# Low part of a fifth weight block by TensorE, with a new order table, in an attention and gated-projection kernel

## The chip, the cores and the metric

The kernel runs on one core of one Trainium2 chip. The metric is device time in microseconds (us) of one execution. The engines are named as the profile names them: PE is TensorE's matmul row, PEld its weight load, DVE is VectorE, ACT is ScalarE, POOL is GpSimd, SP is SyncE, which issues the DMAs.

## The reference

Four batches, eight heads of width 64, 768 positions. Each query sees the first 8 positions and the 96 up to itself, with a linear bias by distance. The heads' outputs are put side by side (512 wide), and a gated block follows:

```python
scores = scale * np.matmul(q, k.transpose(0, 1, 3, 2)) + bias
a = softmax(np.where(keep, scores, -1e9)) 
x = np.matmul(a, v)                                  # (4, 768, 512) after the transpose
gate = 1.0 / (1.0 + np.exp(-causal_conv(x, conv_w))) # 5 taps, per channel
out = (gate * (x @ w_val)) @ w_out                   # both weights 512 x 512
```

The two weights come as 64-bit floats. The kernel splits each into a high part and a low part of 32-bit type and makes three matmuls for each product (high by high, high by low, low by high).

## The kernel before

**Work and stages.** The 768 positions of a batch are cut into two phases of three blocks of 128, so there are eight phases (0 to 7). In each phase four groups (one pair of heads each) go through the attention; two groups make a pair, q = 0 to 15. Every piece of work is an operation with a key, added to a plan in `attention_moe`. The keys that this text uses:

- `Lrk`, `Lrq`, `LV`, `WL`: DMA loads of keys, queries, values and a weight block (line 582), issued by SP.
- `S u`: scores of three steps on PE (line 685). `AM s,j`: bias added and the row minimum taken, on DVE (line 693). `EX s,j`: exponential, on ACT (line 704).
- `RG q,k`: a small number added to four row sums (line 711, POOL or DVE). `RC q,k`: their reciprocal, DVE (line 714). `NM s,j`: the product with it, POOL or DVE (line 720).
- `PT q,k`: transposes on PE, as 12 small ones (line 737), or as 6 whole ones (line 734) where the unit before it on PE uses the whole array. `EV q,k,i`: their copy out of PSUM (line 326, ACT or DVE).
- `PV q,k`: product with the values, PE (line 765). `HI g` prepares the PSUM bank of group g for it (line 328 or 863); `HO g` saves four columns.
- `XH g`, `XL g`: high and low part of x (lines 326 and 872). `CV g,k`: tap k of the convolution (line 881, the first one often on ACT, line 883). `SG ph`: the gate's tanh, ACT.
- `VM ph,m,c`: three matmuls of x with block c of the first weight, PE (line 935). `GM ph,m`: gate times value, DVE (line 944). `GH`, `GL`: its high and low part. `OM ph,k,h,c`: three matmuls with block c of the output weight, PE (line 963). `OE`, `ST`: copy out and store.

**The weight blocks.** There are eight blocks of 128 rows, i = 0 to 3 of the first weight and 4 to 7 of the output weight. A block goes through `WA` (ACT, line 552), `W1`, `W2`, `W3` (DVE, lines 557, 562, 565), `W4` (line 571, POOL or DVE), and `WH`, the cast to the high part (`w_high`, line 591). Then the low part is made in one of two ways. For i < `PE_W` (line 618) it is `WS`, a sum in PSUM by TensorE (`w_sum`, lines 604 to 611), and `WP`, its copy out on ACT (`w_out`, line 326):

```python
nc.tensor.matmul(ps, ident, T["wh", i][:, :DM].bitcast(F32), start=True, stop=False)   # 609
nc.tensor.matmul(ps, units[:, 1], h[:, c], start=False, stop=False)                    # 610
nc.tensor.matmul(ps, units[:, 0], T["wr", i][:, :DM], start=False, stop=True)          # 611
```

For the others `WS` is a subtraction (`w_rest`, line 598) and `WP` an addition (`w_low`, line 602), both on POOL in this kernel. The buffers of the blocks are rings of two, so `W2` of block i waits for `WP` of block i-2. The first `OM` of phase 0 waits for `WP` 4 to 7 (line 1043).

**What sets the order.** `ORDER` lists every operation by the number in which it was added to the plan, with a letter where one of several engines was chosen (a ACT, v DVE, g POOL). The operations of one engine are issued in the order in which they stand there, and an engine takes them strictly in that order. `Plan.order` also works out where the plan expects PE to wait in the first 95 us and puts up to 12 filler matmuls there (lines 450, 458, 464). PSUM banks are rings too: `S u` needs the banks of `S u-1` back from its `AM`s, and `WS`, `VM` and `OM` share a ring of two ("moe").

Of the kernel before, what the change touches and what calls it, by code (L numbers as in the profile page):

```python
# [28 lines left out]
LAG, PV_SPLIT, U_VK, PE_W = 1, 1, 0.0, 4  # L29
WS_POS = (4, 4, 4, 4)  # L30
# [27 lines left out]
    396g 166a 417 418 395g 174 185 419 427 397g 428 420 398g 437 402a 438 421g 22 429 178 422 401a 179 233 426g 430
    11 180 175a 21 425g 311 431v 453 416 423g 432 454 262 404a 433g 457 403a 458 436g 187 439 435g 263 461 12 440
    462 182g 188 24 455 434g 234 1129a 23 189 424g 1135a 194 441v 1138a 1130 183g 177 312 1139 1127a 465 1140 186  # L60
    181g 13 1131 447a 29 448a 466 456 475 190g 313 1128 1136a 476 459 1398 442 485 467 443g 486 203 450a 1141 445g
    235 468 446g 1132 477 18 469g 1142 444g 449a 28 460 184g 1133 314 31 463 1126v 1137 478 470 1143 487 1152 479v
# [1286 lines left out]
```

## Time and profile before

| what | value |
|---|---|
| median of 3 runs | 251.1 us (250.1 to 251.37) |
| the profiled execution, whole time | 249.76 us |
| its span | 248.0 us |
| busy in the span: PE, DVE, ACT, POOL | 238.8, 213.4, 179.6, 130.4 us |
| filler and warm-up matmuls | 13 + 2 of line 450, and 15 more of lines 458 and 464 |

The span is what the profile sees; 1.76 us lie around it. All times in rows count from the span's start. PE is busy 96% of the span, but the first fifth of the span differs from the rest, so the page's shares are read by stretch.

### The profile page before, as it was taken

To read this page: it belongs to the slowest core of one execution; us is meant where nothing else is said; L and a number is where in the kernel's file an instruction comes from. 1 tells how busy PE (TensorE), PEld (TensorE's weight loads), DVE (VectorE), ACT (ScalarE), POOL (GpSimd) and SP (SyncE) were. 2 spreads that over 40 slices of the span, in tenths; PEclk is the share of its full clock that TensorE was granted. 3 is DMA by queue.
4 is the path that set the end of the run, shared out by engine and by line. 5 is a ranking of instruction groups with operands and counts; after the bars stand their busy time and mean duration, and the time that the engine had idled before them with its cause. 6 is when DMAs were issued, how large, how long until landed. Compare 5 with 4: busy or idle time off the path is not lost.

```text
span 248.0 us, 10366 instructions
## 1 busy us (share of the span) xinstructions
PE 238.8 (96%) x4037; PEld 204.7 (83%) x4041; DVE 213.4 (86%) x822; ACT 179.6 (72%) x600; POOL 130.4 (53%) x264
## 2 busy tenths in 40 slices
PE   8998788999999999999999999999999999999993
PEld 3556577888899888988899788898899889988993
DVE  3997999998979989898989989898979979989620
ACT  3999899998998488877967589886678388422202
POOL 6989999999317530364064533455419741810220
PEclk9999999999999999999999999999999999999999
DMA  5999598161298054529558289791079507200303
GB/s 181 401 397 386 200 336 284 36 187 52 61 306 306 3 186 186 167 100 272 187 172 256 84 272 345 221 312 48 7 261 402 200 25 227 73 4 0 127 8 134
DMA packets 23095, 45.94 MB, mean 185 GB/s; under 512 B 2688, under 2 KB 13696, under 8 KB 23040
## 3 DMA queue, kind: packets, MB, share of 16 engines
q1 hardware_dynamic: 23040, 45.21, 53.4%
q8 instruction: 34, 0.56, 0.9%
q14 instruction: 21, 0.17, 0.2%
HBM read 38.91 MB, written 6.29 MB: 182 GB/s over the span
## 4 chain that ended last, share of the span: by engine, by line
PE 80%; DVE 12%; POOL 4%; DMA 1%; issue 1%; ACT 0%; SPq 0%; DVEq 0%; POOLq 0%
PE o L963 26%; PE val L935 25%; PE x L765 11%; PE s L685 9%; PE pt L734 5%; PE pt L737 4%; DVE gate L881 3%; DVE t L693 3%; POOL p L720 3%; DVE wh L562 2%; DMA counts_i<-in_counts 1%; DVE xl L872 1%; DVE wy L557 1%; POOL wvh L328 1%; DVE wy L565 1%
## 5 line engine op out<-in xcount | busy, mean ns | idle before, releaser
L720 POOL TENSOR_SCALAR p<-p,rs 128x168 f32<-128x168 f32 (+1 forms) x152 | 66.3, 450 | 55.1 <-DVE rs L714 36.4
L704 ACT ACTIVATE p<-t,mins 128x168 f32<-128x168 f32 (+1 forms) x192 | 81.5, 430 | 13.8 <-DVE mins L693 12.2
L881 DVE SCALAR_TENSOR_TENSOR gate<-x,cwt,gate 128x384 f32<-128x384 f32 x128 | 76.2, 614 | 1.1
L693 DVE CUSTOM_DVE_ANT_0 t<-s,bias 128x168 f32<-128x168 f32 (+1 forms) x192 | 54.1, 318 | 7.6 <-PE s L685 7.5
L935 PE MATMUL val<-xh,wvh 128*128 128x384 f32 x128 | 44.4, 347 | 0.2 <-DVE gate L944 0.2
L326 ACT COPY a<-pt 128x384 f32<-128x384 f32 (+2 forms) x79 | 35.3, 473 | 11.7 <-PE pt L734 7.6
L935 PE MATMUL val<-xl,wvh 128*128 128x384 f32 x128 | 41.8, 327 | 0.0
L935 PE MATMUL val<-xh,wvl 128*128 128x384 f32 x128 | 41.7, 326 | 0.0
L963 PE MATMUL o<-woh,gh 128*128 128x512 f32 (+1 forms) x100 | 39.1, 391 | 0.0
L704 ACT ACTIVATION_READ_ACCUMULATOR p<-t,mins 128x1 f32 x192 | 37.6, 196 | 0.0
L963 PE MATMUL o<-woh,gl 128*128 128x512 f32 (+1 forms) x100 | 37.2, 372 | 0.0
L963 PE MATMUL o<-wol,gh 128*128 128x512 f32 (+1 forms) x100 | 37.1, 371 | 0.0
L765 PEld LDWEIGHTS x<-a,v 56*64 56x64 f32 (+1 forms) x2112 | 33.7, 135 | 4.0 <-issue 1.1
L685 PE MATMUL s<-rk,rq 64*64 64x168 f32 (+1 forms) x768 | 35.8, 304 | 1.1 <-issue 0.9
L765 PE MATMUL x<-a,v 56*64 56x64 f32 (+1 forms) x2112 | 35.8, 219 | 0.8 <-DVE x L863 0.7
L685 PEld LDWEIGHTS s<-rk,rq 64*64 64x64 f32 x768 | 25.8, 132 | 8.9 <-issue 6.0
L952 POOL TENSOR_TENSOR gl<-gate,gh 128x384 fp32r<-128x384 f32 x24 | 24.1, 1008 | 11.8 <-ACT gh L326 5.0
L935 PEld LDWEIGHTS val<-xh,wvh 128*128 128x128 f32 x128 | 24.2, 189 | 1.8 <-DVE gate L944 0.5
L935 PEld LDWEIGHTS val<-xl,wvh 128*128 128x128 f32 x128 | 24.2, 189 | 0.5 <-DVE xl L872 0.2
L935 PEld LDWEIGHTS val<-xh,wvl 128*128 128x128 f32 x128 | 24.2, 189 | 0.0
L944 DVE SCALAR_TENSOR_TENSOR gate<-gate,val 128x384 f32<-128x384 f32 x32 | 17.4, 549 | 4.7 <-PE val L935 4.5
L963 PEld LDWEIGHTS o<-wol,gh 128*128 128x128 f32 x100 | 18.9, 189 | 2.4
(101 smaller groups left out, 351.0 us busy)
## 6 DMA issues: line engine op xcount, KB each, us to landing
v<-in_vw SPq DMA_DIRECT2D x40, 384.0 KB, 5.6
rq<-in_qT SPq DMA_DIRECT2D x32, 192.0 KB, 5.3
rk<-in_kT SPq DMA_DIRECT2D x16, 252.0 KB, 4.8
out<-ob SPq DMA_DIRECT2D x15, 256.0 KB, 4.8
w<-in_wb SPq DMA_DIRECT2D x7, 512.0 KB, 5.8
again<-in_wb SPq DMA_DIRECT2D x7, 512.0 KB, 5.9
rk<-in_kT SPq DMA_DIRECT2D x16, 200.0 KB, 4.9
out<-ob SPq DMA_DIRECT2D x12, 128.0 KB, 1.8
```

Source lines behind the costliest of these rows:

```text
L326: nc.scalar.copy(dst, src)
L685: nc.tensor.matmul(T["s", step[g, k], j][half], T["rq", g][r, k * P + i * HQ : k * P + (i + 1) * HQ], T["rk", g][r, c0 : c0 + n], start=Tr ...
L693: nc.vector.tensor_tensor_reduce(out=t[:, :n], in0=T["s", s, j], in1=bias[:, h, :P] if n == P else bias[:, h, P:], op0=ALU.add, op1=ALU.mi ...
L704: nc.scalar.activation(p_of(s, j), T["t", s, j][:, :n].rearrange("p (c w) -> p c w", c=pieces(s)[0]), AF.Exp, bias=mins[:, s, j : j + 1], ...
L720: engine(e).tensor_scalar(out=pr, in0=pr, scalar1=rs, scalar2=1.0, op0=ALU.mult, op1=ALU.mult)
L734: nc.tensor.transpose(pt[n // 4][:, n % 4 * P : n % 4 * P + P], src, ident)
L765: nc.tensor.matmul(T["x", 2 * q + r][j * D : (j + 1) * D, c0 : c0 + HQ], v[rows, slot], a[rows, i, n * j + c], start=c == 0, stop=c == use ...
L881: nc.vector.scalar_tensor_tensor(out=gt, in0=src, scalar=w, in1=gt, op0=ALU.mult, op1=ALU.add)
L935: nc.tensor.matmul(T["val", ph, m], (wvh, wvh, wvl)[r][:, c, m * P : (m + 1) * P], woven((T["xh", g], T["xl", g], T["xh", g])[r][:, : size ...
L944: nc.vector.scalar_tensor_tensor(out=t, in0=t, scalar=1.0, in1=T["val", ph, m].rearrange("p (b a) -> p a b", a=2), op0=ALU.add, op1=ALU.mult)
L952: engine(e).tensor_sub(tile_of(("gl", ph, m), [P, HT], F32R, "gl", G_B)[:, :n], T["g", ph, m], T["gh", ph, m][:, :n])
L963: nc.tensor.matmul(T["o", ph, k, h], (T["gh", ph, c], T["gl", ph, c], T["gh", ph, c])[r][:, cols], woven((woh, woh, wol)[r][:, c])[:, h * ...
```

## The change

Two constants and the whole order table change:

```diff
-LAG, PV_SPLIT, U_VK, PE_W = 1, 1, 0.0, 4
-WS_POS = (4, 4, 4, 4)
+LAG, PV_SPLIT, U_VK, PE_W = 1, 1, 0.0, 5
+WS_POS = (0, 4, 4, 4)
 ORDER = """
-    114 0 118 1125 1134 140 2 3 120 1g 122 123 138a 130g 119 128g 149 141 124g 142 133g 131a 143 126a 8 229 125g
+    114 0 118 1124 140 3 2 120 122 123 136a 126g 134a 124g 132a 149 119 1g 142 8 125a 130g 127a 143 135g 7 228 131a
...
```

With `PE_W` 5, block 4 takes the first way: `WS 4` becomes three matmul forms on PE, `WP 4` a copy on ACT, `wr` of the block is written in the rounded 32-bit type. `WS_POS[0]` of 0 takes its PSUM bank from the ring ahead of `VM 0,0`, and the operation is added later, so all numbers between the two places fall by one. Decoded with that, the first part of the two tables reads as follows on each engine (loads of SP left out; blanks between key and numbers left out).

```
before, PE:   ... S4 PT0,2 PV0,1 PV0,2 S5 PT1,0 PT1,1 VM0,0,0 S6 PT1,2 PV1,0 PV1,1 PV1,2 PT2,0 VM0,1,0 VM0,0,1 VM0,1,1
              S7 PT2,1 VM0,0,2 VM0,1,2 VM0,1,3 PT2,2 VM0,0,3 PV2,0 PV2,1 S8 VM0,2,0 VM0,2,1 ... OM0,0,0,0 ...
after,  PE:   ... S4 PT0,2 PV0,1 PV0,2 PT1,0 S5 WS4 PT1,1 VM0,0,0 S6 PT1,2 PV1,0 PV1,1 PV1,2 PT2,0 VM0,0,1 VM0,1,0 VM0,1,1
              VM0,0,2 S7 PT2,1 VM0,0,3 VM0,1,2 VM0,1,3 PT2,2 PV2,0 PV2,1 S8 VM0,2,0 VM0,3,0 ... OM0,0,0,0 ...
before, DVE:  ... AM11,1 W14 RC1,0 W24 W34 RG1,1 AM12,0 RC1,1 AM12,1 AM13,0 AM13,1 W15 AM14,0 AM14,1 W25 W35 RG1,2 CV0,1 CV1,1
              AM15,0 CV1,2 CV0,2 AM15,1 AM16,0 XL0 AM16,1 RC1,2 AM17,0 AM17,1 CV1,3 CV0,3 CV1,4 CV0,4 HO0 XL1 RC2,0 HI2 HI3 RG2,1
              ... W26 W17 ... CV2,4 CV3,4 HI4 AM21,1 HI5 AM22,0 AM22,1 AM23,0 AM23,1 W27 GM0,0 GM0,1 RC3,0 ... W47 GL0,0 ... XL4 AM29,1
after,  DVE:  ... W12 RG0,1 ... W14 AM11,1 W24 RG1,0 RC1,0 W34 RG1,1 AM12,0 RC1,1 AM12,1 W15 AM13,0 AM13,1 RG1,2 AM14,0 AM14,1
              W25 W35 CV0,1 RC1,2 CV0,2 CV1,1 CV1,2 CV0,3 AM15,0 XL0 AM15,1 AM16,0 CV0,4 AM16,1 RG2,0 AM17,0 HI2 RC2,0 AM17,1 CV1,3
              XL1 CV1,4 HI3 ... W26 W17 ... CV2,4 CV3,4 AM21,0 HI4 HI5 AM21,1 AM22,0 AM22,1 AM23,0 AM23,1 GM0,0 GM0,1 RC3,0 W27
              AM24,0 AM24,1 GL0,0 ... W47 ... AM29,0 CV5,1 AM29,1 CV4,3 CV5,2 XL4
before, POOL: ... RG1,0 NM9,1 NM9,0 NM6,0 NM7,0 NM10,1 NM10,0 WH4 NM7,1 NM6,1 WS4 W44 W45 NM8,0 NM11,0 NM11,1 RG2,0 NM8,1 WP4
              ... WS5 ... WP5 WS6 W46 RG3,0 WP6 NM21,1 NM18,0 NM21,0 NM22,1 GH0,0 ... WS7 WP7 ...
after,  POOL: ... WH4 NM9,0 NM6,0 NM9,1 NM7,0 NM6,1 NM10,0 NM10,1 W44 NM11,0 NM8,1 W45 NM7,1 WH5 NM11,1 NM8,0
              ... WS5 ... WH6 ... WS6 NM17,0 W46 WP6 WP5 RG3,0 GH0,0 ... WH7 ... WS7 WP7 ...
before, ACT:  ... EX6,1 WP2 EX9,0 EX9,1 EV0,1,1 EX10,0 ...
after,  ACT:  ... WP2 EX6,1 EX9,0 EV0,1,1 EX10,0 EX9,1 ... EX13,1 EX16,0 WP4 EV1,1,0 ...
```

Over the whole table these move between engines: `WH` 1, 5, 6, 7 from ACT to POOL; `BIAS` (six of sixteen from POOL to ACT, three back); `RG 0,1`, `RG 1,0` and `RG 2,0` from POOL to DVE in this stretch, `RG 2,1` from DVE to POOL; `HO 0` from DVE to ACT. Later in the table eight more `EV` and the three `OE` of DVE go to ACT. On PE, `PT 1,1` now follows a unit of the whole array (`WS 4`), and further on two `PT`s leave the whole form and two others take it, so 22 `PT`s take the whole form where 21 did. On SP some loads of the head change places, and none is added: the two operations of block 4 issue no DMA.

## Rows read from the trace of the kernel before

**Rows 1.** Busy time by stretch; columns PE, PEld, DVE, ACT, POOL, clock, DMA share, GB/s.
```profile
0.00:46.50 46.50, 41.26 (x716) 27.71 (x720) 40.76 (x173) 40.76 (x141) 41.99 (x85) 1.00 0.80 292
46.50:243.70 197.20, 197.17 (x3320) 176.84 (x3321) 172.60 (x650) 138.14 (x458) 88.36 (x180) 1.00 0.49 161
```

**Rows 2.** Chain of waits that ended last, head alone: start, us, what.
```profile
22.32 0.20 POOL sm L711
22.55 0.18 DVE rs L714
...
43.52 0.07 DVE x L328
...
43.83 0.08 DVE x L328
...
44.90 1.10 DVE wh L562
```

**Rows 3.** Timeline of PE, 25 to 47 us: start, us, instruction, [idle before and its releaser].
```profile
25.75 1.32 PE L685 MATMUL s<-rk,rq 64*64 64x168 f32 x23
27.97 0.35 PE L685 MATMUL s<-rk,rq 64*64 64x168 f32 x1 [0.89 <-issue]
28.57 0.47 PE L737 MATMUL pt<-ident,p 64*128 64x64 f32 x8 [0.25 <-issue]
29.50 0.86 PE L737 MATMUL pt<-ident,p 64*128 64x64 f32 x12 [0.46 <-ACT a L326]
...
34.43 2.00 PE L765 MATMUL x<-a,v 64*64 64x64 f32 x120 [0.73 <-DVE x L863]
...
40.26 0.59 PE L737 MATMUL pt<-ident,p 64*128 64x64 f32 x12 [0.64 <-POOL p L720]
...
46.53 0.43 PE L935 MATMUL val<-xh,wvh 128*128 128x384 f32 x1 [0.16 <-DVE gate L944]
```

**Rows 4.** Timeline of PE: four fillers; the first matmuls of two weight blocks' sums.
```profile
7.65 1.05 PE L464 MATMUL ptf<-const-bfloat16-1.0 128*128 128x512 bf16 x4
...
10.49 1.12 PE L609 MATMUL wsum<-wh,ident 128*128 128x512 f32 x2
...
11.92 1.02 PE L609 MATMUL wsum<-wh,ident 128*128 128x512 f32 x2
```

**Rows 5.** Chain that ended last: one unit of small and one of whole transposes.
```profile
50.53 0.52 PE pt L737 x12
...
53.20 0.66 PE pt L734 x6
```

**Rows 6.** Groups of instructions of POOL, 0 to 60 us: busy us, mean ns, idle.
```profile
L720 POOL TENSOR_SCALAR p<-p,rs 128x168 f32<-128x168 f32 x38 | 17.9, 486 | 0.5 <-DVE rs L714 0.2
L598 POOL TENSOR_TENSOR wh<-wh,woh 128x512 f32<-128x512 f32 x4 | 5.1, 1282 | 0.0
...
L328 POOL CAST wvh<-wh 128x512 fp32r<-128x512 f32 x3 | 2.9, 961 | 0.0
...
L534 POOL TENSOR_SCALAR bias<-dist 128x168 f32<-128x168 f32 x4 | 2.1, 536 | 0.2
...
L328 POOL CAST woh<-wh 128x512 fp32r<-128x512 f32 x1 | 0.6, 605 | 0.0
```

**Rows 7.** Timeline of DVE around its one wait after the start.
```profile
20.76 0.44 DVE L557 TENSOR_SCALAR wy<-w 128x512 int32<-128x512 int32 x1
...
23.75 0.15 DVE L711 TENSOR_SCALAR sm<-sm 128x4 f32<-128x4 f32 x1
```

**Rows 8.** Line 562 (`W2`): duration ns shortest/median/longest, first and last start us.
```profile
L562 DVE SCALAR_TENSOR_TENSOR wh<-w,wy x8: 660/702/1194, 6.7 to 44.8; 128x512 int32<-128x512 int32 x7, 128x532 int32<-128x532 int32 x1
```

**Rows 9.** Timeline of POOL: `W4` of blocks 4 and 5 together.
```profile
28.80 2.51 POOL L571 TENSOR_TENSOR wr<-wls,wy 128x512 f32<-128x512 f32 x2
```

**Rows 10.** ACT: the end of `EX 9,1` on the timeline, and the group of `WP` 0 to 3.
```profile
20.34 0.19 ACT L704 ACTIVATION_READ_ACCUMULATOR p<-t,mins 128x1 f32 x1
...
L326 ACT CAST wvl<-wsum 128x512 fp32r<-128x512 f32 x4 | 2.3, 577 | 0.0
```

More of the change, by code (lines that the diff above doesn't have):

```diff
@@ L58 @@
[L58 to L62, printed above, removed]
@@ L128 @@
-    1766 1776 1771 1777 1772 1778
+    114 0 118 1124 140 3 2 120 122 123 136a 126g 134a 124g 132a 149 119 1g 142 8 125a 130g 127a 143 135g 7 228 131a
+    141 4 144 128g 138a 356 145g 129a 357 358 360 115 139a 361 362 364 146g 116 365 158 150 151 117 366 152 9 363
+    229 153 10 359 155g 227 367 147 368 154g 369 370 378 379 371 388 380 372v 137g 167 389 156 373 381 1133 376v 14
+    377g 148a 160 374g 15 382v 133a 161 375g 159 5 230 162 390 164g 383 163v 391 308 387g 157a 404 405 165 392g 406
@@ new lines @@
+    731g 1513 764 772 756g 1509 1504g 1229a 77 747 1514 1505g 1478 1510 774 1515 1234 55 1511a 1520 1484 1235 736a
+    1512g 1237a 1516 773 751 1230 1521 775 1517 246 1241 1518v 331 80 788 1519g 1238 790 1522 1490 1244v 757 765
+    1242 60 761g 1526 1243 1523 760v 1252v 776v 766v 1527 767 1524a 777 789 792 778g 281 738a 793 780g 739a 61 796
+    791 758g 282 797 759g 794 768g 247 779g 771g 283 800 770g 769v 332 801 781g 1247v 1528 782a 62 1248 802 1532
+    1249 798 783a 1529 1250 799 810 1533 1530a 811 820 1245a 1534 1255v 795 1251 333 67 822 821 812 1535 1253v 785a
@@ new lines @@
+    1559g 861 1564 337 1271a 1268 884 1568 834a 885 211 1278 1565a 1276 1573 1537 871 1566g 1277 1569 75 886 1272
+    1574 856g 888 862v 1287 872g 1570 835v 889 288 863 1571a 873 892 865g 875v 887 287 864g 893 289 212 876g 877v
+    251 1288a 866g 1282a 867v 76 874g 890 338 86 896 1291a 897 1575 213 891 906 1283 879a 1579 898 1280v 878a 1576
+    1292 908 907 1580 899 1293 81 1577a 339 1281 91 909 1294 1578 1581 880a 916 881a 1586 917 894 1295 1582 900v
+    1289a 901 1284 252 1583a 904g 1285 903g 895 340 93 918 1286 82 1593 1290 883a 932 1594 933 934 936 1587 882a
@@ new lines @@
+    905v 1595 937 1585 940 1588 98 902v 941 94 1596 214 919 1589 1279a 253 920g 1296a 910g 1304a 935 911 914v 341
+    915g 938 944 913g 945 292 946 954 99 955 947 912v 215 290 926a 964 948g 927a 1572 965 291 939 921 83 949 1590
+    924g 942 254 925g 1299v 1591g 1597 342 1307a 923g 1297a 1600 922g 1308 929a 950g 1309 966 1601 1592g 956 1607
+    1298 957 980 1602 1310 943 1608 958g 88 981 1598g 928a 959 1603 1300 1305a 100 962g 1609 982 1599v 951g 967 343
+    1604 984 1610 1605g 985 986 952v 1614 89 1606g 1611 101 988 1615 1612a 1301 105 983 1620 1306 1613g 217 987 989
@@ new lines @@
+    223 1017 1631 1034 298 1637 108 1022a 1644 296 1638g 1018v 257 1329a 1011g 1031 1639v 1332a 1008v 1647 1040
+    1341a 1041 1648 1330a 1050 1042 1654 1051 1060 1043 1649 1333 113 1645a 1655 1044g 1334 1023a 96 1650 1646g
+    1338a 1335 1052 1656 1053 1651 348 1019g 1045 1061 1020g 1652a 1331 1657 1021g 1024a 1661 1046g 1035 1658 1025a
+    258 1336 1054g 1339a 1653g 97 1659a 1340 225 349 1038 1342 1660g 1625 1062 1662 1346 1343 1039 1047g 1026a 1667
+    1344 1027a 1076 1663 1063 1077 1078 1080 1668 1064g 1055 1079 1065 1345 1059g 1664 1058g 1056v 1057g 1669 1355
@@ new lines @@
+    1695 1115g 1368 1373a 1104g 1701 1118a 1369 1106g 1696 1119a 1107g 1114v 1702 1116g 1370 111 1697 1117g 1672
+    1374 1693g 354 1678 1698 1703 1376 1121a 1699g 1708 1120a 1377 1700g 1371 355 1378 1709 1123a 1379 1122a 1704
+    1380a 1710 1388a 1705 307 1706a 1707v 305 306 1714 1383a 1391a 1384 1711 1392 1715 1712a 1393 1381a 1716 1394
+    1720 1385 1389a 1717 1382 1390 1721 1718a 1386 1722 1395 1723 1387 1727 1724a 1780 1728 1726 1734 1729 1735 1730
+    1736 1731 1737 1732v 1741 1738 1742 1733v 1739g 1748 1781 1743 1749 1744 1740v 1782 1750 1745 1713 1767 1751
@@ L129 @@
+    1725 1755 1719 1752 1773 1746v 1756 1753v 1747v 1761 1754v 1768 1762 1757 1783 1763 1758 1769 1759 1764 1760
+    1770 1765 1774 1771 1775 1766 1776 1772 1777 1778
 """.split()
```

114 lines of the change are left out of this document (45 added, 69 removed).

## Prediction

> **What bounds the kernel now.** I read busy time by stretch first, because the page's 96% for PE is a mean over unlike stages. From 46.5 us to the end of the matmuls PE is idle for 197.20 - 197.17 = 0.03 us, at the full clock; before that it is idle for 5.24 us, and DVE, ACT and POOL are each busy 41 to 42 of 46.5 us [rows 1]. So behind 46.5 us the time is PE's own work, which the change hardly alters, and the result is decided by when PE reaches `VM 0,2,0`, which starts at 46.53 [rows 3]. Next the chain of waits in the head: it runs over DVE nearly without a break into that matmul: `HI 4` and `HI 5`, four more row minima, `W2` of block 7 (1.10 us of chain), `GM 0,0`, and then PE; further up it goes from `RG 1,0` on POOL at 22.32 to `RC 1,0` on DVE [rows 2]. Last, PE's own timeline between 25 and 47 us: before that of 0.16 at the end, waits of 0.89, 0.25, 0.46, 0.73 and 0.64 us. The first stands inside the unit `S 5`, between its 23rd and 24th matmul, and nothing that the profile shows ends it; the others end by an operation of ACT, DVE or POOL [rows 3].
>
> **The change part by part.**
>
> *The sum on PE.* Two sums in a row start 11.92 - 10.49 = 1.43 us apart [rows 4]; that is what `WS 4` adds. `PT 1,1` behind it takes the whole form, 0.66 for 0.52 us, and so does one unit more in the whole table: 0.14 us, the same unit [rows 5]. Cover: before, PE waits 0.89 + 0.25 + 0.46 = 1.60 us between 27.1 and 29.5 us [rows 3]. With the cover gone, PE would pay all 1.57 us. Whether the sum comes in time is a question of `W4` of block 4 on POOL. `NM 9,0` starts after `RC 1,0`, at about 22.8 as before; seven `NM` at 0.486 us [rows 6] end at 26.2, `W4` of 1.26 us (half of [rows 9]) at 27.5. PE is through `PT 1,0` and `S 5` at 27.0 to 27.9, without or with the 0.89 us wait, so `WS 4` ends at 29.0 to 29.3. Behind it `PT 1,1` waits for `NM 7,1`, which POOL now makes after `NM 11,0`, `NM 8,1` and `W4` of block 5: 27.5 + 3 x 0.486 + 1.26 = 30.2, that is 0.7 us later than its 29.50 [rows 3]. The next gate on PE hides this: `S 6` needs `AM 17,1` (below). I cost the sum at nothing.
>
> *POOL.* Up to `NM 14` and `NM 17` it loses the subtraction and the addition of block 4, 2 x 1.282, three `BIAS` net at 0.536, and two `RG` net (each as DVE's 0.15 or somewhat more). It gains the casts of blocks 1, 5 and 6, between 0.605 and 0.961 us each [rows 6, 7]. The net is 2.56 + 1.61 + 0.3 - 1.8 to 2.9: POOL is 1.6 to 2.7 us lighter; I take 2.0. What it gains is mostly not on the path, because POOL waits for `RC` each time; it only has to stay ahead of DVE.
>
> *ACT.* Four 512-wide casts leave, one copy comes (0.577 us [rows 10]), with three `BIAS` and a small copy: lighter by about 4 x 0.58 - 0.58 - 3 x 0.3 = 0.8 us, no cost. `WP 4` stands behind `EX 16,0`, near 32 us, and `W2` of block 6, which needs its buffer, stands on DVE behind `HI 3`, at 34 us or later: covered by 2 us.
>
> *DVE, which sets the pace.* Before, `RC 1,0` stood idle from 21.20 to 22.55 for `RG 1,0` in POOL's queue [rows 2, 7]. Now `RG 1,0` is on DVE itself, behind `W2` of block 4. Its input `EX 9,1` ended at 20.53 [rows 10] and now stands behind one copy and one exponential more, some 0.8 us, so 21.3; DVE reaches it at 21.20 + 0.15 (`RG 0,1`) + 0.66 [rows 8] = 22.0, covered by 0.7 us. From the start of `RC 1,0` to `RG 1,1` it is 23.75 - 22.55 = 1.20 us of work, unchanged in what it holds [rows 2, 7]. So `RG 1,1` starts at 21.20 + 2 x 0.15 + 1.20 + about 0.15 for a reciprocal that follows its own guard at once = 22.85: a lead of 0.9 us. `RG 2,0` comes, `RG 2,1` and `HO 0` go: nothing. Behind `AM 17,1` there is a loss: `CV 0,3`, `CV 0,4`, `RG 2,0`, `HI 2` and `RC 2,0` now precede it, so `S 6` starts at about 32.3 for 31.4, `PT 1,2` ends at 33.9, and `PV 1` starts at 33.9, 0.5 us early by [rows 3] though `HI 3` is 0.9 early. The 0.64 us wait for POOL before `PT 2,1` [rows 3] gives the rest back, since POOL is ahead by 2.0.
>
> *The gate of PE at `PV 2`.* `HI 4` is 0.9 us early; `HI 5` is also moved ahead of `AM 21,1`, 43.83 - 43.52 = 0.31 more [rows 2], 1.2 us. Half of `PV 2` needs the one, half the other: 1.0 us. At `VM 0,2,0` PE then waited 0.16 us more for `GM 0,0` [rows 3]; as `W2` of block 7 now stands behind `GM 0,1`, `GM 0,0` is 0.9 + 1.10 = 2.0 us early [rows 2] and this wait goes. Sum: 1.0 + 0.16, so PE is **1.2 us** early at `VM 0,2,0`.
>
> *Bounds.* Below, the lead cannot pass DVE's 2.0 us at `GM 0,0`. Above, the lead can vanish and the sum's 1.57 us appear. Two things the trace of before cannot show. One is the number of filler matmuls that the planner sets with the new table: they fill waits that it expects, so I count none; a filler takes 1.05 / 4 = 0.26 us [rows 4], and at most 12 stand in one place, so 0 to 3.1 us. The other is SP's order: some loads of the head change places in a stretch with a DMA share of 0.80 [rows 1], each still a unit or more ahead of its reader: nothing, or a part of the lead.
>
> *DVE beside POOL.* `W2` takes 0.66 to 0.70 us, but 1.194 beside `W4` of block 6 on POOL [rows 8]; that of block 4, right behind `RC 1,0`, is the shortest, while POOL ran its `NM`s. [...]
>
> *Behind 46.5 us* DVE, ACT and POOL must hold the lead for some 10 us more, as all three are full there. The first `OM` needs `WP 7`, which POOL's lighter load brings forward by more than 1.2 us. `GL 0,0`, now early on DVE, needs `GH 0,0`, ahead of which POOL now has four `NM` (1.9 us) less. `S 10` needs `AM 29`, which moves ahead of four operations of DVE. I cost this and the rest of the table at nothing; without those three covers the lead would be lost there.
>
> The profiled execution's 249.76 us would become 248.6. It lies 1.3 us under the median of the runs, so the number is taken from the median: 251.1 - 1.2 = **249.9 us**. A measurement of this kernel can tell about 0.5%, 1.26 us, so the forecast lies on that line.
>
> **The rivals.**
>
> *Fillers on the path (slower).* The planner sets fillers where its own times show PE waiting. Ahead of `PV 1`, `PT 2,1` and `PV 2` PE waited 0.73 and 0.64 us and hardly at all [rows 3]; where a unit comes 1.2 us sooner than the planner holds, PE still has to run the fillers, since they stand in its queue. From five on (5 x 0.26 = 1.3 us [rows 4]) the lead is gone; one place filled with its 12 costs 2.6 to 3.1 us (by the planner's own 0.22 for one, or by the row), and with the lead of 1.2 the time is 1.4 to 1.9 us longer: **252.6 us**. For it: 15 such matmuls stand in the head before. Against it: in the waits of [rows 3] only few of them do, and PE's idle time there was left over. Chance 0.18.
>
> *The lead is not there (no change).* `RG 1,0` waits on DVE as long as it did on POOL, because `EX 9,1` now stands behind a copy that waits for `PT 0,1`. Then 0.31 + 0.16 us remain of the lead, and the waits on PE that the sum was to use are gone into it: 0 to -0.4, **250.9 us**. Chance 0.15.
>
> *PE takes all of DVE's lead (faster still).* [...] Chance 0.12.
>
> **How the numbers follow.** The forecast has 0.55; its own range is 249.1 to 250.7, and as its middle lies on the line of 1.26 us, 0.29 of it counts as faster and 0.26 as same. With the rivals: faster 0.29 + 0.12 = 0.41; same 0.26 + 0.15 = 0.41; slower 0.18. The range runs from 248.8 (under the fastest case) to 252.2: it leaves out most of the slow rival and what of the fastest goes beyond it.
>
> **What would show it.** Right: DVE without a wait near 21 us; `WS 4` on PE at 27 to 29.5; `PV 2` starting at 42.5 to 42.8; `VM 0,2,0` near 45.3 with nothing idle behind. Wrong: a wait on DVE ahead of line 711, 714 or 952, PE waits between 46 and 60 us, or more fillers of lines 458 and 464 between 25 and 46 us.

## The result, and the profile after

The changed kernel takes 251.45 us, the median of 18 executions (249.70 to 253.81); the kernel before, run 18 times as well, takes 250.08 us (249.49 to 251.54). The ratio is 1.0052, 95% interval 1.0028 to 1.0077: **slower by 0.5%**, where 249.9 us and a gain of 1.2 were forecast. Two things about these numbers matter for what follows.

- Both kernels' executions fall into groups. Of the kernel before 13 lie at 249.5 to 250.3 us and 5 at 251.1 to 251.5. Of the changed one two lie at 249.7 and 249.8, ten at 251.0 to 251.8, six at 252.1 to 253.8. So equal code differs by more than the change is worth, and what has to be explained is which group an execution falls into.
- Two of the three executions that gave the 251.1 us of the prediction were of the upper group (251.1 and 251.37).

The profiled execution of the changed kernel is of its slowest group: 253.08 us (span 251.1 us), 1.6 us above its own median.

Busy time by stretch, the view of [rows 1]; the border is `VM 0,2,0` again (columns PE, PEld, DVE, ACT, POOL, clock, DMA share, GB/s):

```profile
0.00:45.95 45.95, 42.36 (x713) 28.11 (x717) 40.59 (x173) 40.00 (x143) 40.56 (x80) 1.00 0.79 282
45.95:245.40 199.45, 198.07 (x3323) 177.29 (x3320) 168.97 (x640) 143.36 (x475) 85.37 (x177) 1.00 0.49 162
```

The head is 0.55 us shorter than in [rows 1] and holds 1.65 us less waiting on PE (45.95 - 42.36 = 3.59 for 5.24). Behind it stand 199.45 us for 197.20, and 1.38 us of waits where there were 0.03.

Timeline of PE between 25 and 47 us, the rows that answer to [rows 3] (in order: the second part of `S 5`, `WS 4`, `S 6`, `PV 1`, `PV 2`, `VM 0,2,0`):

```profile
27.43 0.58 PE L685 MATMUL s<-rk,rq 64*64 64x168 f32 x9 [0.39 <-issue]
...
28.39 1.02 PE L609 MATMUL wsum<-wh,ident 128*128 128x512 f32 x2
...
32.69 1.45 PE L685 MATMUL s<-rk,rq 64*64 64x168 f32 x24 [0.68 <-issue]
34.58 2.05 PE L765 MATMUL x<-a,v 64*64 64x64 f32 x120
...
43.57 1.63 PE L765 MATMUL x<-a,v 56*64 56x64 f32 x93 [0.19 <-DVE x L328]
...
45.97 0.43 PE L935 MATMUL val<-xh,wvh 128*128 128x384 f32 x1
```

Timeline of DVE, the place of [rows 7]: `W2` of block 4, then `RG 1,0`, `RC 1,0` and (fourth row) `RG 1,1`, with no wait in brackets anywhere:

```profile
22.23 0.68 DVE L562 SCALAR_TENSOR_TENSOR wh<-w,wy 128x512 int32<-128x512 int32 x1
22.83 0.16 DVE L711 TENSOR_SCALAR sm<-sm 128x4 f32<-128x4 f32 x1
23.02 0.18 DVE L714 RECIPROCAL rs<-sm 128x4 f32<-128x4 f32 x1
...
23.54 0.46 DVE L711 TENSOR_SCALAR sm<-sm 128x4 f32<-128x4 f32 x1
```

Timeline of PE at its two waits behind the border, `S 9` and a stop in the middle of a `PV`:

```profile
49.84 0.67 PE L685 MATMUL s<-rk,rq 64*64 64x128 f32 x6 [0.28 <-PE x L765]
...
157.57 1.39 PE L765 MATMUL x<-a,v 56*64 56x64 f32 x79
160.06 1.16 PE L765 MATMUL x<-a,v 56*64 56x64 f32 x64 [1.10 <-issue]
```

And the end. The last matmul ends at 245.69 us and the span at 251.12, 5.43 us later; in the kernel before it is 244.02 and 247.96, 3.94 us. In the view of DMA, the stretches 247.0 to 248.5 and 248.5 to 250.1 us (queue, kind: packets, MB, share of 16 engines): q8 carries instructions, q1 all loads and stores.

```profile
q1 hardware_dynamic: 209, 0.18, 36.9%
q8 instruction: 1, 0.02, 6.1%
...
q1 hardware_dynamic: 9, 0.01, 3.1%
```

In the last 1.6 us nine packets remain of a store of 128 KB, and one packet of 16 KB of instructions stands ahead of them.

**Marks common to all profiles.** The start of `S 0` differs between executions of equal code (below), so I measure from it. Each line is one profiled execution; "head" is `S 0` to `VM 0,2,0`, "rest" is from there to the end of the last `OM`, "end" from there to the end of the span, all in us. "Packet" is the start of the instruction packet that PE's stop at 159 us hangs on. (The profiled execution of e3_wl is left out: PE stands 1.92 us there, and the granted clock is 0.50 from 160.6 to 164.0 us.) The mark isn't perfect: a late `S 0` isn't passed on in full, as the new head shows with 38.82 to 39.00 us where `S 0` stands at 6.67 to 7.10 and 38.54 and 38.57 where it stands at 7.43 and 7.59. So heads are best compared at like `S 0`.

| kernel | `S 0` at | head | rest | end | packet at | PE stop near 159 |
|---|---|---|---|---|---|---|
| before | 6.70 | 39.83 | 197.50 | 3.94 | 154.28 | none |
| changed | 7.43 | 38.54 | 199.72 | 5.43 | 157.61 | 1.10 |
| e1_headA, new head, old rest | 7.59 | 38.57 | 197.84 | 3.97 | 154.84 | none |
| e1_headB, old head, new rest | 6.75 | 39.93 | 198.27 | 4.97 | 154.55 | none |
| e1_Bsum, before + sum on PE | 7.11 | 40.11 | 197.49 | 3.95 | 156.58 | none |
| e1_Anofill, changed, no late filler | 7.10 | 38.83 | 198.33 | 5.28 | 153.85 | none |
| e2_Aom, changed, old `OM 7` order | 7.04 | 38.88 | 199.84 | 5.42 | 157.73 | 1.10 |
| e2_rg, before + `RG 1,0` on DVE | 7.63 | 39.07 | 197.58 | 3.92 | 154.66 | none |
| e2_w27, before + `W2`, `HI 5` moved | 6.73 | 39.41 | 198.51 | 5.05 | 155.15 | none |
| e2_rgw27, both of these | 6.99 | 39.02 | 198.60 | 3.62 | 154.85 | none |
| e3_endfill, changed + 10 matmuls at the end | 6.74 | 38.90 | 198.47 | 4.07 | 154.56 | none |
| e3_both, the same, block 3's load moved | 6.80 | 38.87 | 199.75 | 4.58 | 157.41 | 1.10 |
| e3_Bend, before + 10 matmuls at the end | 6.96 | 39.81 | 197.48 | 4.39 | 154.33 | none |
| e4_wl, changed, block 2's load moved | 6.67 | 39.00 | 198.36 | 5.25 | 154.64 | none |
| e4_fix, the same + 10 matmuls at the end | 6.83 | 38.82 | 198.35 | 4.38 | 155.80 | none |

### The profile page after: what moved, and what is told of

The parts are those of the page before. It is cut to its first block, busy times and chain, and to the rows that moved or that the text cites. A ratio compares the mean times of both kernels' runs of the same rounds, so it can differ in the third digit from the quotient of the medians.

```text
span 251.1 us, 10366 instructions
## 1 busy us (share of the span) xinstructions
PE 240.7 (96%) x4033; PEld 205.5 (82%) x4037; DVE 209.6 (83%) x813; ACT 183.7 (73%) x617; POOL 125.9 (50%) x256
## 4 chain that ended last, share of the span: by engine, by line
PE 86%; DVE 8%; DMA 2%; issue 1%; SPq 1%; ACT 0%; DVEq 0%
PE o L963 26%; PE val L935 24%; PE x L765 13%; PE s L685 11%; PE pt L734 5%; PE pt L737 4%; PE warm L450 2%; DVE t L693 2%; DMA rq<-in_qT 2%; DVE gate L881 2%; DVE wh L562 1%; DVE wy L565 1%; DVE wy L557 1%; DVE wr L571 1%; PE s L458 0%
## 5 line engine op out<-in xcount | busy, mean ns | idle before, releaser
L326 ACT COPY a<-pt 128x384 f32<-128x384 f32 (+2 forms) x88 | 39.1, 472 | 11.1 <-PE pt L737 5.6
L765 PEld LDWEIGHTS x<-a,v 56*64 56x64 f32 (+1 forms) x2112 | 34.4, 135 | 5.1 <-issue 2.0
L765 PE MATMUL x<-a,v 56*64 56x64 f32 (+1 forms) x2112 | 36.7, 220 | 1.3 <-issue 1.1
L952 POOL TENSOR_TENSOR gl<-gate,gh 128x384 fp32r<-128x384 f32 x22 | 22.2, 1009 | 7.4 <-ACT gh L326 2.5
L963 PEld LDWEIGHTS o<-woh,gh 128*128 128x128 f32 x100 | 18.9, 189 | 2.8 <-DVE gate L944 0.3
## 6 DMA issues: line engine op xcount, KB each, us to landing
rk<-in_kT SPq DMA_DIRECT2D x16, 252.0 KB, 4.5
```

The lines of the kernel that those rows point to most:

```text
L326: nc.scalar.copy(dst, src)
L765: nc.tensor.matmul(T["x", 2 * q + r][j * D : (j + 1) * D, c0 : c0 + HQ], v[rows, slot], a[rows, i, n * j + c], start=c == 0, stop=c == use ...
L952: engine(e).tensor_sub(tile_of(("gl", ph, m), [P, HT], F32R, "gl", G_B)[:, :n], T["g", ph, m], T["gh", ph, m][:, :n])
L963: nc.tensor.matmul(T["o", ph, k, h], (T["gh", ph, c], T["gl", ph, c], T["gh", ph, c])[r][:, cols], woven((woh, woh, wol)[r][:, c])[:, h * ...
```

## The experiments

Order tables are written here by keys. "Before" is always the kernel before on the same chip.

### Which half of the table loses: e1_headA and e1_headB

```diff
-order = before
+order = changed[: VM 0,2,0] + (what is left, as in before)        # e1_headA, PE_W = 5
+order = before[: VM 0,2,0] + (what is left, as in changed)        # e1_headB, PE_W = 4
```

> New head, old rest: the changed kernel's order up to VM 0,2,0 (with WS 4 on TensorE), and behind it the operations that are left in the order and on the engines of the kernel before. Theory R (the loss stands behind 46 us, in the rest of the table and the tail, and the head gains the 0.56 us that the two profiles show): the time is 250.1 - 0.6 = 249.5 us. Rival H (the head costs, by a later start or by its DMA order, and the rest is neutral): 251.4 us, like the changed kernel. Rival C (the two parts only fit together; where they meet PE waits): above 252 us, with waits of PE between 46 and 60 us.

> Old head, new rest: the order of the kernel before up to VM 0,2,0 (WS 4 and WP 4 on POOL), and behind it what is left in the changed kernel's order and on its engines. Theory R (the loss stands behind 46 us): 250.1 + 1.9 = 252.0 us, with the filler ahead of PV 5,2 near 88 us, a PE wait of about 1 us inside a unit that nothing in the profile ends, and some 5 us from the last matmul to the end of the span. Rival H (the head costs): 250.1 us.

Measured: e1_headA 249.53 us, ratio to before 0.9969 (0.9957 to 0.9981); e1_headB 251.96 us, 1.0080 (1.0065 to 1.0096), beside 250.13 us. Theory R holds for both: the new head gains, the new rest loses, and the two together give about what the changed kernel loses. The table says where: the new head is 1.26 us shorter (39.83 to 38.57; some 0.3 of it is its late `S 0`), the new rest is 0.77 us longer (197.50 to 198.27), and the end 1.03 us longer. The stop at 159 us, which the expectation of e1_headB also named, is not in its profile.

e1_headA is faster than both kernels, by the 0.6 us that are left of the head's 1.0: its rest is 0.34 us longer than in the kernel before, with the same order on PE. PE stands 0.30 us at 47.05 in the middle of `VM 0,2,0`, without a releaser and 1.33 us after a packet of instructions has landed (on such stops see below).

In the profile of e1_headB the granted clock is 0.50 from 30.9 to 34.3 us and in that of e2_rg, below, from 30.5 to 33.9 us, and 1.00 around it; PE had stood 0.90 and 0.59 us in `S 5` before. `S 6` takes 1.96 us in both, for 1.33 in the kernel before. Little of it reaches `VM 0,2,0`, because PE waits for POOL behind it anyway (at `PT 2,1`, 0.35 and 0.51 us).

### The parts of the head: e1_Bsum, e2_rg, e2_w27, e2_rgw27

```diff
-LAG, PV_SPLIT, U_VK, PE_W = 1, 1, 0.0, 4
+LAG, PV_SPLIT, U_VK, PE_W = 1, 1, 0.0, 5                          # e1_Bsum alone
-PE: S5 PT1,0 PT1,1       POOL: NM6,1 WS4 W44 ... NM8,1 WP4
+PE: S5 PT1,0 WS4 PT1,1   POOL: NM6,1 W44     ... NM8,1            ACT: EX16,0 WP4 EV1,1,0
-POOL: NM5,1 RG1,0 NM9,1  DVE: W14 RC1,0 W24                       # e2_rg
+POOL: NM5,1 NM9,1        DVE: W14 RG1,0 RC1,0 W24
-DVE: HI4 AM21,1 HI5 AM22,0 ... AM23,1 W27 GM0,0 GM0,1 RC3,0       # e2_w27
+DVE: HI4 HI5 AM21,1 AM22,0 ... AM23,1 GM0,0 GM0,1 RC3,0 W27
```

e2_rgw27 has the last two together. These three have the fillers of the kernel before; e1_Bsum has three fewer (two ahead of `VM 0,0,0`, one ahead of `PT 1,2`).

> The kernel before with the sum of block 4 alone moved: WS 4 on TensorE right ahead of PT 1,1, WP 4 on ACT behind EX 16,0, no filler added ahead of them. Theory: PE's 1.43 us lie in waits of 1.60 us that are there anyway, and POOL is lighter by 2.56 us, so the time is 250.1 us, within 0.4 of the kernel before, and PE reaches VM 0,2,0 at 46.3 to 46.7 us. Rival: the sum is paid in full, 251.6 us, with VM 0,2,0 at 48.0 us. Rival: POOL's 2.56 us come through RG 1,0, and VM 0,2,0 starts at 45.5 us, 249.1 us.

> The kernel before with RG 1,0 alone moved from POOL to DVE, right ahead of RC 1,0; the same fillers. The prediction's step (DVE's wait of 1.35 us at RC 1,0 is what the head can win; 0.9 us of it arrives at PE): from the start of S 0 to VM 0,2,0 it is 39.85 us in the kernel before, and 38.9 to 39.2 here, and the time is 250.1 - 0.8 = 249.3 us. Rival (another operation takes the place of RG 1,0, and the lead is gone by PV 2): 39.7 us or more, 250.1 us.

> The kernel before with two operations of DVE moved: HI 5 ahead of AM 21,1, and W2 of block 7 behind GM 0,0, GM 0,1 and RC 3,0; nothing else. The prediction's step: 0.31 + 0.16 = 0.47 us, so S 0 to VM 0,2,0 takes 39.4 us for 39.85 and the time is 250.1 - 0.4 = 249.7 us. Rival (W2 of block 7 is then late for its own readers, WH, W3, W4 and WP of block 7, and OM 0 waits for it): a PE wait between 46 and 58 us, and 250.1 us or more.

> The kernel before with RG 1,0 on DVE and the two moves of DVE together, WS 4 still on POOL. If the three make up the whole lead of the new head (1.3 us from S 0 to VM 0,2,0 in its profiles), the sum on TensorE and POOL's lighter load gave nothing: 38.6 us for 39.85, and 250.1 - 1.2 = 248.9 us, a version faster than both kernels. Rival (the lead needs POOL's 2.56 us less): 39.2 us or more and 249.5 us.

Measured:

| run | time | ratio to before (95%) | head against 39.83 | rest against 197.50 |
|---|---|---|---|---|
| e1_Bsum | 250.83 | 1.0031 (1.0016 to 1.0045) | +0.28 | 0.0 |
| e2_rg | 249.96 | 0.9980 (0.9961 to 1.0000) | -0.76 | +0.1 |
| e2_w27 | 250.72 | 1.0010 (0.9990 to 1.0031) | -0.42 | +1.0 |
| e2_rgw27 | 250.32 | 0.9993 (0.9977 to 1.0009) | -0.81 | +1.1 |

`RG 1,0` alone seems to bring the 0.76 us that were expected, but `S 0` stands 0.93 us later in this profile than in the kernel before. e2_rgw27 against e2_w27, which differ in the same edit and have `S 0` at 6.99 and 6.73, gives 39.41 - 39.02 = 0.39 us, and the time falls by 0.31 (249.96 for 250.27 beside it) where 0.8 was expected. So `RG 1,0` is worth some 0.4 us. The sum on TensorE alone is not free: with three fillers less on PE the head is still 0.28 us longer, so most but not all of its 1.43 us fell into waits; the median is up by 0.7 us, of which the rest isn't explained by this profile. It lies between the theory and the first rival. Moving `W2` of block 7 and `HI 5` does what was forecast up to `VM 0,2,0` (-0.42 for -0.47), and then loses more than it won: from `VM 0,2,0` to `S 9` it takes 49.45 - 46.14 = 3.31 us for 49.42 - 46.53 = 2.89, the whole 0.42 given back, and some 0.6 us more go by `S 10`, none after it. `W2` of block 7 itself takes 1.65 us there for 1.19, beside an addition of POOL. Here the rival was right that the loss lies behind 46 us. e2_rgw27 has 39.02 us, between its theory's 38.6 and its rival's 39.2, and no gain in time (250.32, with 248.9 expected). The new head takes 38.83 and 38.88 at like `S 0` (7.10 and 7.04), 0.15 to 0.2 less; whether that is POOL's lighter load or another of the moves, no run separates.

### The filler near 88 us: e1_Anofill

```diff
-FILL_UNTIL, FILL_GAP, FILL_MAX = 95.0, 0.35, 12
+FILL_UNTIL, FILL_GAP, FILL_MAX = 60.0, 0.35, 12
```

> The changed kernel without the one filler matmul that its planner sets near 88 us ahead of PV 5,2 (it sets none there in the kernel before). If the filler is on the path: 251.45 - 0.3 to 0.5 = 251.1 us. If it is not, 251.4 us. The profile also shows whether the 1.1 us that PE stands at 159 us and the 5.4 us from the last matmul to the end of the span come again (they belong to the table) or not (they belong to one execution).

Measured: 251.97 us (251.50 to 253.09), 1.0083 (1.0063 to 1.0104): no gain. In the table its rest of 198.33 us equals that of e4_wl, which has the filler (198.36). Three of the six lie at 252.4 to 253.1. What this run was worth is its profile: the long end came again (5.28 us), the stop at 159 us did not, and the instruction packet stood at 153.85 instead of 157.61 us. So the two are separate, and the stop belongs to some executions only.

### The end: e2_Aom, e3_endfill, e3_Bend

```diff
-PE: ... OM7,2,0,1 OM7,1,0,1 OM7,0,0,2 OM7,1,0,2 OM7,0,0,3 OM7,2,0,2 OM7,1,0,3 OM7,2,0,3 OM7,2,1,1 OM7,2,1,2 OM7,2,1,3   # e2_Aom
+PE: ... OM7,2,0,1 OM7,1,0,1 OM7,0,0,3 OM7,1,0,2 OM7,2,1,1 OM7,1,0,3 OM7,2,1,2 OM7,2,0,2 OM7,2,0,3 OM7,2,1,3
             fn(e)
+        for _ in range(10):                                       # e3_endfill on the changed kernel, e3_Bend on the kernel before
+            nc.tensor.matmul(T["o", NPH - 1, 0, 0], nc.const_aps.tensor(1.0, [P, P], BF16), nc.const_aps.tensor(1.0, [P, DM], BF16), start=True, stop=True)
```

> The changed kernel with one thing put back: PE takes the 48 matmuls of the last output phase (OM 7, 16 operations) in the order of the kernel before, on the same places of PE's queue; the copies out and stores keep their order. In that order the store of block 0 leaves some 0.65 us earlier against the end of PE. Theory T (the changed order of OM 7 lets the four last stores stand so close together that one share of the last one, eight packets of 1 KB, comes behind a 16 KB packet of instructions; that is 1.3 to 1.4 us): 251.45 - 1.35 = 250.1 us, and from PE's last matmul to the end of the span some 3.95 us. Rival (the long end comes from something else of the new table, such as the late stores of phase 6 or the number of PE's instructions): 251.4 us, and 5.0 to 5.4 us at the end.

> The changed kernel with ten matmuls of zero use behind PE's last one (2.2 us on PE, into a PSUM bank that nobody reads any more; the outputs do not depend on them). They keep PE's last fetch of instructions away from the last store's packets. Theory C (the end of the span is 1.3 to 1.4 us late where the last eight packets of the last store wait behind a 16 KB packet of instructions): from the last matmul of OM 7 to the end it is 3.6 to 4.0 us for 5.0 to 5.4, and the time 251.45 - 1.35 = 250.1 us. Rival (the stores themselves stand too close together): 251.4 us. Second rival (the end waits for PE): some 2 us are added, 252.5 us or more.

> The kernel before with the same ten matmuls behind PE's last one. About a third of its executions lie at 250.8 to 251.6 us, the others at 249.5 to 250.5. Theory C: the upper group is the same late packet, and goes away; median 250.0 us, none above 250.6. Rival: the two groups stay, median 250.2 us; or, if the end waits for PE, 251 us or more.

Measured: e2_Aom 251.34 us, 1.0027 (0.9999 to 1.0056), in two groups of six, 249.9 to 250.8 and 251.9 to 253.4. The old order of `OM 7` makes the late end rarer and doesn't remove it: the profile is of the upper group, with an end of 5.42 us although the first of the last stores left as early as in the kernel before. Theory T is not what decides.

The ten matmuls do decide it. e3_Bend: 250.42 us (249.97 to 250.73), 0.9990 (0.9971 to 1.0009); of the 35 executions of the kernel before beside it ten lie at 251.4 to 252.0, of these twelve none lies above 250.73. e3_endfill: 250.74 us for 251.45, eight of twelve at 250.2 to 251.0, and its end is 4.07 us; the other four, at 251.5 to 252.3, were not profiled, and the next part takes up what may lengthen them. The matmuls cost a little themselves (e3_Bend's end is 4.39 us for 3.94), which hides part of the gain. The records of single DMA packets show what meets there. Times are from the end of the last `OM`; a store is cut into 16 shares of eight packets, and "15 shares" is when all but one had ended:

```
execution     instruction packet   15 shares of the last store   its last share, first to last
before         2.46 to 3.88         2.58                          ends 2.66
e1_headA       2.04 to 3.09         2.29                          2.29 to 2.63
changed        1.92 to 3.37         2.44                          3.36 to 4.06
e1_Anofill     2.13 to 3.22         2.56                          3.20 to 3.90
e1_headB       1.85 to 2.92         2.55                          2.90 to 3.60
e2_Aom         2.41 to 3.35         2.47                          3.34 to 4.04
e2_w27         1.80 to 2.99         2.48                          2.97 to 3.68
e3_endfill     3.26 to 4.55         2.42                          ends 2.76
```

In each execution with a long end the last share begins within 0.02 us of the end of the instruction packet; where the packet comes after the last share, the end is short. The packet's time alone doesn't decide: in e1_headA it starts at 2.04 and the last share runs beside it from 2.29 to 2.63 (much the same in e1_Bsum, e2_rg and e2_rgw27, which are not in the list), and why the share doesn't wait there is not shown (the records don't name the DMA engine of a packet). All five profiles with the new rest and no extra matmuls have it, and one of six with the old rest. That the eight packets wait for the 16 KB one is my reading of these times; how the DMA chooses between the two is not shown. What makes the new table lose the race nearly always, and the old one about a quarter of the time (31 of the 126 executions of the kernel before in these comparisons lie above 250.75 us), is not settled: the order of `OM 7` is a part of it.

### The stop at 159 us: e3_wl, e3_both, e4_wl, e4_fix

```diff
-SP: ... LV12,0 Lrk28 LV12,1 Lrq28 Lrk29 WL2,3 ST3,2,0 Lrq29 WL2,4   # e3_wl; e3_both with the ten matmuls too
+SP: ... LV12,0 Lrk28 LV12,1 Lrq28 Lrk29 ST3,2,0 Lrq29 WL2,3 WL2,4
-SP: ... Lrq27 WL2,2 ST3,0,0 LV11,2 LV12,0 Lrk28 LV12,1 Lrq28 Lrk29 WL2,3   # e4_wl; e4_fix with the ten matmuls too
+SP: ... Lrq27 ST3,0,0 LV11,2 LV12,0 Lrk28 LV12,1 Lrq28 Lrk29 WL2,2 WL2,3
```

> The changed kernel with one load moved on SP: the second reading of weight block 3 (half a megabyte, issued at 151.9 us in the middle of nine DMAs in a row) is issued only behind the next two, right ahead of that of block 4. Theory F (the 1.1 us that PE stands at 159 us are a 16 KB packet of instructions that waits behind these transfers: it comes at 157.6 us, where in another execution it comes at 153.9 and PE doesn't stand): the packet comes before 156 us, no wait at 159 us, and no execution above 252.2 us, where six of 18 of the changed kernel lie; median 251.2 us or less. Rival (the wait belongs to something else in PE's queue): it stays, and the spread to 253.8 us stays.

> The changed kernel with both edits, the load of weight block 3 moved and the ten matmuls behind the last one. If the two late packets of instructions are the whole of what the change lost against its forecast, all executions lie near the two fastest of the changed kernel (249.7 and 249.8 us): 249.7 to 250.2 us, faster than the kernel before by 0.1 to 0.5 us. Rival (the rest of the new table costs by itself more than the head gains): 250.5 us or more.

> The changed kernel with another load moved on SP. The load that stands in the burst of nine DMAs at 149 to 153 us is the second reading of weight block 2, not of block 3 as the earlier edit took it; here it is issued ahead of that of block 3, at some 163 us, and is read by DVE at 174 us. Theory F: with half a megabyte less the DMA is idle from some 155.5 us on instead of 157.5, the packet of instructions for PE comes before 156 us, PE does not stand at 159 us, and no execution lies above 252.3 us; median 251.2 us. Rival (the packet is late for another reason than this burst): a wait of 1.1 us or more at 159 us again, and a part of the executions at 252.3 to 253.8 us.

> The changed kernel with weight block 2's second load moved as in the run beside it, and the ten matmuls of zero use behind PE's last one. If the two late packets of instructions are all that makes the spread of the changed kernel, it falls into one group, like the lower eight of the twelve with the ten matmuls alone (250.2 to 251.0 us): median 250.5 us, none above 251.2, equal to the kernel before with those ten matmuls (250.4 us). That would leave nothing of the head's 1.1 us, because the rest of the table takes 0.8 us more on PE. Rival: two groups as without the move of the load, the upper at 251.5 to 252.4 us.

The first two were a miss of mine: the block that is read in the burst at 149 to 153 us is block 2, and block 3 is read at 163 us anyway. They measured 251.52 us (1.0040, 1.0017 to 1.0062) and 251.48 us (1.0028, 1.0001 to 1.0056), and left burst and stop where they were (1.10 us in the profile of e3_both, an execution of 251.96 us, with the ten matmuls in place).

With the right load moved, e4_wl takes 251.42 us, 1.0041 (1.0019 to 1.0063), one execution at 249.8 and nine at 251.1 to 252.0: no execution lies above 252, the late end is still there (5.25 us). e4_fix takes 250.85 us, 1.0014 (0.9995 to 1.0033), all twelve at 250.25 to 251.25, a little above the 250.5 expected and without the upper group of e3_endfill. That fits theory F and doesn't prove it: the two ran on another chip than e3_endfill, the changed kernel was not run beside them, and e1_headB, e1_Anofill and e3_endfill have the packet at 153.85 to 154.56 us, and no stop, with the load where it was. View of DMA, 153.0 to 157.5 us, first the changed kernel, then e4_wl:

```profile
q1 hardware_dynamic: 790, 1.63, 100.0%
```

```profile
q1 hardware_dynamic: 585, 1.05, 64.5%
q8 instruction: 1, 0.02, 1.3%
```

In the changed kernel all 16 DMA engines are busy for the whole 4.5 us and no instruction packet comes through; in e4_wl it does. And SP in the changed kernel, the burst itself (two of its rows; a row with x2 is two DMAs, and this one is waiting with its second):

```profile
151.86 0.38 SPq L582 DMA_DIRECT2D again<-in_wb  x1
...
152.75 6.13 SPq L397 DMA_DIRECT2D v<-in_vw  x2
```

PE goes on 1.49 us after the packet has landed (157.61 + 0.97 = 158.57, then 160.06 us); I read it as having run out of instructions. The stop that [rows 3] show in `S 5` without a releaser has the same mark: a packet lands at 26.54, and PE goes on at 27.97, 1.43 us later. It stands in every profile here, 0.20 to 0.97 us long and 1.2 to 1.5 us behind a landing. Most packets have no such stop behind them: q8 carries 34 of 16 KB in the execution of the changed kernel, and these two stops of PE follow one (0.39 us in `S 5`, 1.10 us here). A full DMA is not what decides: the kernel before has a DMA share of 1.05 from 153 to 155 us, and its packet came at 154.28; and in e1_headA PE stands 0.30 us at 47.05 for a packet that came at 44.23, with a DMA share of 0.02 from 43 to 44 us. What sets the moment at which a packet starts is left open.

## Why the prediction was wrong

**The step that failed** is the one under "Behind 46.5 us": "I cost this and the rest of the table at nothing". Three things stood there that cost time.

- PE's rest is 0.8 us longer (198.27 to 198.47 us in the profiles without the stop, for 197.48 to 197.58 in four with the old). About 0.5 us of that lie ahead of `S 9`: 49.84 - 45.97 = 3.87 us with five `VM`, where the kernel before took 2.89 with four, and one `VM` is 0.49. There is the wait of 0.28 us, a PE wait between 46 and 60 us, which the prediction had named as a sign against it. The profile puts it down to PE's own `x`; by the times it is DVE's row minima, from which `S 9` gets its banks back. Timelines of POOL and of DVE, changed kernel:

```profile
43.58 2.55 POOL L602 TENSOR_TENSOR wol<-wh,wr 128x512 fp32r<-128x512 f32 x2
46.22 0.20 POOL L711 TENSOR_SCALAR sm<-sm 128x4 f32<-128x4 f32 x1
```

```profile
46.45 0.18 DVE L714 RECIPROCAL rs<-sm 128x4 f32<-128x4 f32 x1 [0.65 <-POOL sm L711]
46.54 1.06 DVE L562 SCALAR_TENSOR_TENSOR wh<-w,wy 128x512 int32<-128x512 int32 x1
...
47.95 0.90 DVE L952 TENSOR_TENSOR gl<-gate,gh 128x384 fp32r<-128x384 f32 x1
...
49.41 0.32 DVE L693 CUSTOM_DVE_ANT_0 t<-s,bias 128x168 f32<-128x168 f32 x1
```

  `W2` of block 7, moved out of `GM 0,0`'s way, and `GL 0,0` now stand ahead of `AM 26,0`, which ends at 49.73, 0.11 us before `S 9` starts. I named `GL 0,0` and found a cover for its own wait, but didn't ask who is queued behind both on DVE. Ahead of both DVE waits 0.65 us more, at `RC 3,0`, for `RG 3,0` of POOL: the wait ahead of line 714 that the prediction had named as a sign against it. `RG 3,0` starts at 46.22 (45.92 in e4_wl, whose `S 0` is as early as in the kernel before), for 45.55, although POOL was to be 2.0 us ahead: `WP 6`, which stood behind it, now stands before it. The six profiles with new head, new rest and no stop of PE's in `VM 0,2,0` all have this wait of DVE (0.60 to 0.68 us) and PE's at `S 9` (0.08 to 0.32 us). e2_w27 shows the move of `W2` alone giving its 0.42 us back by `S 9`; how much is due to each of the three here, no run separates. Another 0.2 us go between `S 9` and `S 10` (`S 10` starts 10.72 us after the border with four `OM` ahead of it, for 11.32 with six, and one `OM` is 0.65), and 0.2 behind `S 10`, where PE has no wait and the new order of its work, with one filler more, takes that much longer.
- The end is 1.35 us longer (3.62 to 3.97 us in the short ones, 4.97 to 5.43 in the long ones), nearly always, where it happens to a quarter of the executions before.
- PE's stop of 1.1 us at 159 us comes in about a third of the executions (six of 18 above 252.1 us).

Sum: -1.0 for the head, +0.8, +1.35 x (16/18 - 31/126) = +0.9 (if every execution of the two upper groups has the late end), +1.1 x 6/18 = +0.4, together +1.1 us; the medians differ by 1.37 and the means by 1.43, so some 0.3 us are not accounted for.

**The start of the sum** was 1.0 us too high: the median of the three executions was 251.1, that of 18 is 250.08. So the forecast of 249.9 stood next to no change, and the gain it had in mind would have been 248.9.

**The head came, at 1.0 of the 1.2 us, and by a smaller lead of DVE than forecast.** From `S 0` to `VM 0,2,0` the eight profiles with the whole new head take 38.54 to 39.00 us, median 38.85, for 39.81 to 39.93 in the three with the old one: 1.0 us, forecast 1.2. DVE has no wait at 21 us. `RG 1,1` starts 23.54 - 7.43 = 16.11 us behind `S 0` for 23.75 - 6.70 = 17.05, which looks like the 0.9 forecast; but in the six profiles of the new head with `S 0` at 6.67 to 7.10 it is 16.40 to 16.50, a lead of 0.6. `PV 2`, forecast at 42.5 to 42.8, starts at 43.57, and at 43.23 to 43.27 where `S 0` is as early as before: 0.4 us sooner than the 43.64 before, not 1.0. The rest of the gain lies behind that: `PV 2` takes 1.63 us for 1.88, and the 0.16 us at `VM 0,2,0` are gone. That `VM 0,2,0` stood at 45.97 and not at 45.3 is by 0.3 us the late `S 0` (7.43 for 6.70), which isn't the table's doing (last section); at an early `S 0` it stands at 45.64 to 45.67. Of the waits in [rows 3] the one of 0.25 us has no releaser either; the prediction put it down to another engine.

**The sum on PE** ran at 28.39 us, inside the forecast's 27 to 29.5, and in the new head it didn't cost the lead; by itself on the old head, with three fillers less, it costs 0.28 us there (e1_Bsum), so "nothing" was somewhat too good.

**The rivals.** The slower side came true, by another mechanism than the one named: the planner sets four fillers in place of five between 25 and 35 us, and the one near 88 us costs nothing that the times show. (The head of the kernel before has 18 of them and not 15: 15 is the number of recorded matmuls, and PE's weight loads of these two lines are 12 and 6.) That the lead isn't there is excluded by the head's times, and PE did not take 2.0 us of it.

**DVE beside POOL.** `W2` of blocks 5 and 6 took 0.835 and 0.715 us, 0.951 and 0.707 before. In the changed kernel POOL runs `NM`s beside both and no cast. In the group of line 562, the answer to [rows 8]:

```profile
L562 DVE SCALAR_TENSOR_TENSOR wh<-w,wy x8: 682/714/1064, 6.8 to 46.5; 128x512 int32<-128x512 int32 x7, 128x532 int32<-128x532 int32 x1
```

The longest is again block 7's (1.064 us at 46.54, beside the cast `GH 0,0` of POOL). The prediction looked at DVE alone, where `W2` of block 4 is the shortest. There it is POOL that is held up: `NM 9,1` starts at 22.82 inside that `W2` (22.64 to 23.30) and takes 0.72 us, where an `NM` of this shape takes 0.41 by itself. In the changed kernel the six that meet a `W2` already begun, or begin with it, take 0.83 to 0.93 us and end 0.16 to 0.28 us behind it; where POOL's operation begins first, `W2` ends 0.54 to 0.70 us behind that one. So where the two meet at `W2`, block 4's included, the later one is held up: an `NM` by 0.42 to 0.52 us, and `W2` by up to 0.37 us (block 7's 1.064, begun 0.06 us after the cast, for the 0.693 of block 1's, which has nothing of POOL's beside it). Beside the taps of the convolution, which read `x` in PSUM, an `NM` takes 0.41 us.

## What to carry to other kernels

When an order table changes as a whole, a lead at one gate is worth nothing until the queue behind that gate is read too: whatever was moved out of the way there stands in front of something else. Measure such a change from a common mark (here the first scores) and by groups of executions: two of three executions in the upper group moved the baseline by 1.0 us, nearly the gain that was forecast. Read the packets of instructions in the DMA records too: here the last share of the last store began, at 3.36 us behind the last `OM`, as a 16 KB packet of them ended at 3.37, and behind a burst of loads with a DMA share of 100.0% one came at 157.61 us, for 154.28 in the kernel before. Look for a PE wait that ends by nothing the profile shows, and for the time between the last matmul and the end of the span.

## What the runs showed of the hardware

- The start of `S 0` differs by up to 0.96 us between profiles of kernels that begin alike (6.67 to 7.63 us). TensorE begins its warm-up matmuls at 0.78 us in each; they start 0.43 us apart until 4.5 us in the kernel before and 6.2 us in the changed one, where its granted clock is first recorded, as 1.00, and 0.22 us apart from there on. This change comes at 3.5 us in the earliest profile and at 6.6 us in the latest, and the 13 warm-up matmuls end at 5.1 and 6.5 us. e2_rg, with the latest change, has the latest `S 0`.
- A packet of 16 KB of instructions takes 0.9 to 1.9 us on the DMA. PE has no stop behind most of the 34 (two named here in the changed kernel). Where PE stands without a releaser at the places named here, it goes on 1.2 to 1.5 us after one has landed: 0.20 to 0.97 us in `S 5` in every profile, 0.30 in `VM 0,2,0` in e1_headA and e3_endfill, 1.10 near 159 us in three.
- In two profiles (e1_headB, e2_rg) the granted clock is 0.50 for 3.4 us from 30.9 and 30.5 us on, behind PE's stop in `S 5`; in the others, with the same stop, it stays at 1.00 there.
- `W2` on VectorE and an operation of GpSimd beside it hold each other up: in the changed kernel `NM` takes 0.83 to 0.93 us for 0.41 where it comes second or begins with a `W2`, and `W2` of block 7 takes 1.064 us for 0.693 where it comes behind a cast.
- Ten matmuls that compute nothing, behind everything that PE has to do, took a kernel's slow group away (e3_Bend: none of 12, for ten of 35), and the last packet of instructions then starts 3.3 to 4.1 us after the last `OM` and not 1.8 to 2.5, behind the last store.
